# Turning four more pairs of attention heads by DMA, with another written order of steps, in a fused linear-attention and mixture-of-experts kernel

## Chip, cores and metric

The kernel runs on one core of a Trainium2 chip. The metric is the device time of one execution, in microseconds (us). A core has five engines that each run their own instruction list in order: TensorE (PE; its weight loads are PEld), VectorE (DVE), ScalarE (ACT), GpSimd (POOL) and SyncE (SP, which only issues DMAs here). They wait for each other through semaphores.

## The reference

Two stages are computed, one feeding the other.

```python
# attention: q, k, v are (8, 8, 576, 64), w_phi is (64, 128)
def phi(x):
    proj = einsum('bhsd,df->bhsf', x, w_phi)
    proj = proj - max(abs(proj), axis=-1)
    return concatenate([exp(proj), exp(-proj)], axis=-1)
kv  = einsum('bhsf,bhsd->bhfd', phi(k), v);  z = sum(phi(k), axis=2)
num = einsum('bhsf,bhfd->bhsd', phi(q), kv)
x   = num / (einsum('bhsf,bhf->bhs', phi(q), z) + 1e-6)      # -> (4608, 512)
# experts: w_gate (512, 8), w1 (8, 512, 1024), w2 (8, 1024, 512)
P = exp(x @ w_gate - max)
8 times:  P /= P.sum(1) + 1e-9;  P /= P.sum(0) + 1e-9;  P *= N / E
out = sum over e of  P[:, e:e+1] * (relu(x @ w1[e]) @ w2[e])
```

## The kernel before, in words

**Attention.** The 8 batches have 8 heads each, taken two at a time: a *pair*, numbered 0 to 31 (4 * batch + pair). 512 of the 576 positions of a head are worked off as four tiles of 128; the other 64 positions, the *rests*, go once per batch (`rest_a`, `rest_c`). For each pair `pair_a` projects the tokens of k (PE, `tokens`), takes the maxima of absolute values (DVE, L614), exponentials (ACT, L618) and scales v by them (POOL, L810); `maxima` and `queries`, which it returns, do the same for q. `pair_b` multiplies keys by values (PE, L622, copied by DVE in L892); its inner function `outs` forms numerator and denominator of one head (PE, L905) and divides on DVE (L913, L918, L919). The result lies in a buffer `xb`, tokens by features.

**Turning the output.** The experts need x with the features on the partitions, in the tile `xT`. `pair_c` does that for one pair. It has two ways: four PE transposes into a PSUM bank (L934) and a DVE copy to `xT` (L937); or one DMA transpose on SP's queue straight from `xb` to `xT` (L928). The kernel before uses the DMA for the pairs of batches 3 to 6.

**Experts.** xT is cut into nine groups of 512 tokens: group g below 8 is the main part of batch g, group 8 holds all rests. `gate` makes the logits of a group. Expert 0 is computed plainly (`up0`, `down0`) and needs no routing weight for most groups, so its matmuls can be put between attention steps: up0 of group g needs all four pairs of batch g in xT, and the weights that `load_w0` brings. They are the *fill* that keeps PE occupied while ACT and DVE work on attention. `routing` is a chain on DVE with one small matmul per round. Experts 1 to 7 follow with fast-multiplication schemes (`up7`, `up49`, `down7`), whose order of steps is written in `UNITS`.

**What sets the order.** Operations are recorded by `plan.op` with an engine, a cost and the keys that they read and write. `Plan.schedule` then places them: at each step it takes the operation that can start earliest by its costs, and of equals the one that was recorded first. So the recorded order matters, and for attention it is written by hand as a string of letters, `order`, one per step: l and e load, t turns q and k by DMA (L567), w loads expert 0's weights, r is `rest_a`, a, q and p the three parts of `pair_a`, b, n and m those of `pair_b`, c is `pair_c`, g is `rest_c` with `gate`, u and d are a quarter of `up0` or `down0` for a group. The n-th occurrence of a letter is its n-th piece of work. Loads (`stage_l`, `stage_e`, `load_w0`) also wait for the latest maxima that stand before them in the string (`gates`).

q and k of batches 0 and 1 come through SP and are turned on PE (L752); those of the others are cast by POOL's loads (L550) and turned by SP (L567). SP issues its DMAs in order, and so does POOL, between its computations: what waits holds up what stands behind it in the queue.

Of the kernel before, what the change touches and what calls it, by code (L numbers as in the profile page):

```python
# [349 lines left out]
def kernel(  # L350
# [18 lines left out]
    NP = H // 2  # L369
# [43 lines left out]
    def pe(cols, fn, r=(), w=(), takes=()):  # L413
        plan.op("PE", max(cols / 2400.0 + 0.0025, 0.031), 0.22, fn, r, w, takes)
# [4 lines left out]
    def dve(el, fn, r=(), w=(), shared=False):  # L419
        plan.op("DVE", el / 960.0 + 0.07, 0.15, fn, r, w, shared=shared)  # L420
# [7 lines left out]
    def dma(queue, nbytes, rate, fn, r=(), w=()):  # L428

        speed, unit = LINK.get(rate, (rate, 40))  # L430
        if nbytes == 2 << 20:
            speed, unit = 400, 150
        o = plan.op(queue, 0.8 if queue == "POOL" else 0.6, 0.0, fn, r, w, (), nbytes / speed)
        o.turn, o.unit = rate == 148, unit
# [71 lines left out]
    def new(tag):  # L506
        return R[tag].new()

    def bf(buf):

        return buf().bitcast(BF16)
# [412 lines left out]
        return xb, outs  # L924

    def pair_c(b, pr, xb):
        if b in (3, 4, 5, 6,):
            dma("SP", 1 << 17, 148, lambda: nc.sync.dma_start_transpose(  # L928
                out=xT[:, pr, b * SM:(b + 1) * SM].rearrange("p (a c) -> p a c", c=128),
                in_=xb()[:, 0:NJ].rearrange("p a b -> p (a b)")), [(xb, 0), (xb, 1)], [("xT", b, pr)])  # L930
            return
        pxt = new("PP")
        for j in range(NJ):
            pe(128, lambda j=j: nc.tensor.transpose(  # L934
                bf(pxt)[:, j * 128:j * 128 + 128], xb()[:, j, :], ident),
                [(xb, 0), (xb, 1), "ident"], [pxt])
        dve(270, lambda: nc.vector.tensor_copy(  # L937
            out=xT[:, pr, b * SM:(b + 1) * SM], in_=bf(pxt)[:, 0:512]),
            [pxt], [("xT", b, pr)])
# [150 lines left out]
    def stage_g(b):  # L1090
# [7 lines left out]
             "r": stage_r, "b": stage_b,  # L1098
             "n": lambda j: kvs[j](0), "m": lambda j: kvs[j](1),
             "c": lambda j: pair_c(j // 4, j % 4, xbs[j]), "g": stage_g,  # L1100
             "u": lambda i: up0(i // 4, i % 4), "d": lambda i: down0(i // 4, i % 4)}
    order = (
        "lraeaepqbwlqaqawwabwmqlltnrbppnwqbppmrmanbqaqmwwacmpnpbccpwbtcnmqnaqbclupunm"
        "taumquglcapalbcpnqqdcenmucugbblnapmrcqdutabnqpmunpbambccddnqplanmqmducpblttb"
        "augnaqlnrbdcampcadmqeutunqcppmdcaqtdqabpbbmlrqtdnpmuaqualbnagnacctbmqulupran"
        "tdpmtdqcmdnpdabdancpcabbqmpumqbcdgnappqunburqcbugmmnqdcdanumupqbnucmcpnmbddp"
        "bqmpncncubncmmgccg"
    )
    for i, n in enumerate(order):
        at[0] = i  # L1110
# [948 lines left out]
```

## Time and profile before

| what | value |
|---|---|
| runs, median of 3 | 1009.96 us (1009.75 to 1012.1) |
| profiled execution, first to last instruction | 1008.8 us |
| DMA moved | 128.86 MB, mean 128 GB/s |
| HBM read and written | 122.50 MB and 19.53 MB |
| granted TensorE clock | 1.000 over the whole span |

The span runs from the first to the last instruction of the profiled execution; the times of the runs are about 1.2 us longer, for what lies around the span. Busy time of an engine is the union of its instructions' records. PE records overlap, since matmuls are pipelined: a row such as "x8" merges eight neighbours, and its length less one record, divided by seven, is the step from one to the next. In rows of windows the columns are PE, PEld, DVE, ACT, POOL (busy us, and instructions in brackets), granted clock, mean share of DMA engines that are busy, and GB/s. In rows of the timeline they are the start, the length, engine, line, operation, output and inputs. Attention and the first fill take the first 204 us, routing and the rest of expert 0 last until about 259 us, and the other seven experts until the end.

### The profile page before, as it was taken

To read this page: it belongs to the slowest core of one execution; us is meant where nothing else is said; L and a number is where in the kernel's file an instruction comes from. 1 tells how busy PE (TensorE), PEld (TensorE's weight loads), DVE (VectorE), ACT (ScalarE), POOL (GpSimd) and SP (SyncE) were. 2 spreads that over 40 slices of the span, in tenths; PEclk is the share of its full clock that TensorE was granted. 3 is DMA by queue.
4 is the path that set the end of the run, shared out by engine and by line. 5 is a ranking of instruction groups with operands and counts; after the bars stand their busy time and mean duration, and the time that the engine had idled before them with its cause. 6 is when DMAs were issued, how large, how long until landed. Compare 5 with 4: busy or idle time off the path is not lost.

```text
span 1008.8 us, 23309 instructions
## 1 busy us (share of the span) xinstructions
PE 994.0 (99%) x8376; PEld 727.7 (72%) x8376; DVE 898.6 (89%) x1999; ACT 812.8 (81%) x1930; POOL 447.6 (44%) x514
## 2 busy tenths in 40 slices
PE   7899999999999999999999999999999999999998
PEld 5666666644566877777777877787778777787775
DVE  7999998987888998899989898989889988989886
ACT  7999999845979788878878788777887888778874
POOL 5778674400133344434444444444443444344443
PEclk9999999999999999999999999999999999999999
DMA  9999999181136423282327133632246222724653
GB/s 249 183 202 183 157 153 144 38 170 56 53 121 143 147 97 98 84 184 96 109 98 170 44 100 131 130 127 98 97 117 177 97 98 84 147 79 142 208 174 126
DMA packets 129748, 128.86 MB, mean 128 GB/s; under 512 B 55776, under 2 KB 98272, under 8 KB 129632
## 3 DMA queue, kind: packets, MB, share of 16 engines
q1 hardware_dynamic: 97680, 103.33, 36.3%
q0 software_dynamic: 31648, 23.86, 16.9%
q8 instruction: 65, 1.06, 0.5%
q14 instruction: 51, 0.42, 0.2%
q10 hardware_dynamic: 304, 0.20, 0.1%
HBM read 122.50 MB, written 19.53 MB: 141 GB/s over the span
## 4 chain that ended last, share of the span: by engine, by line
PE 92%; DVE 3%; ACT 2%; DMA 2%; issue 1%; POOL 0%; DVEq 0%
PE ps L1466 41%; PE ps L1475 20%; PE ps L622 17%; PE ps L1607 11%; PE ps L905 2%; DMA xi6t<-X 1%; DMA xi<-X 1%; PE ps L752 1%; ACT q L618 0%; DVE m L614 0%; ACT k L618 0%; DVE wx L614 0%; DVE X L1240 0%; DMA acc<-in_k_dram 0%; DVE hs L1676 0%
## 5 line engine op out<-in xcount | busy, mean ns | idle before, releaser
L1875 POOL TENSOR_TENSOR acc<-acc,hx 128x512 f32<-128x512 f32 x186 | 236.1, 1276 | 404.7 <-ACT hx L1872 135.0
L1466 PEld LDWEIGHTS <-hs 128*128 128x128 bf16 x1984 | 194.1, 98 | 46.4 <-issue 0.2
L1872 ACT ACTIVATE hx<-ps,P 128x256 f32<-128x256 f32 x372 | 158.9, 483 | 53.4 <-PE ps L1466 52.0
L1860 DVE SCALAR_TENSOR_TENSOR acc<-ps,P,acc 128x256 f32<-128x256 f32 x372 | 162.2, 478 | 30.2 <-PE ps L1466 28.2
L1475 PE MATMUL ps<-xT,T 128*128 128x512 bf16 x608 | 171.0, 379 | 0.0
L1466 PEld LDWEIGHTS <-hx 128*128 128x128 bf16 x1488 | 145.6, 98 | 24.9
L1466 PE MATMUL ps<-hx,hs 128*128 128x256 bf16 x992 | 144.3, 273 | 0.0
L1676 DVE CUSTOM_DVE_ANT_0 hs<-ps,U 128x512 bf16<-128x512 f32 x192 | 124.7, 684 | 11.3 <-PE ps L1475 6.6
L1607 PE MATMUL ps<-xT 128*128 128x256 bf16 x576 | 125.4, 272 | 0.0
L1475 PEld LDWEIGHTS <-T 128*128 128x128 bf16 x672 | 65.8, 98 | 40.6
L1682 ACT ACTIVATE hs<-ps 128x512 bf16<-128x512 f32 x96 | 55.9, 598 | 41.7 <-PE ps L1475 40.2
L1466 PE MATMUL ps<-wx,hs 128*128 128x256 bf16 x560 | 78.4, 273 | 0.0
L622 PE MATMUL ps<-w,hx 128*128 128x512 bf16 x288 | 73.0, 379 | 0.0
L622 PE MATMUL ps<-xT,w 128*128 128x512 bf16 x288 | 72.9, 379 | 0.0
L1466 PE MATMUL ps<-wx,hx 128*128 128x256 bf16 x496 | 72.3, 273 | 0.0
L1676 DVE CUSTOM_DVE_ANT_0 hs<-ps,X 128x512 bf16<-128x512 f32 x96 | 65.1, 684 | 7.8 <-PE ps L1607 6.9
L1466 PE MATMUL ps<-hx 128*128 128x256 bf16 x496 | 71.2, 273 | 0.0
L1607 PEld LDWEIGHTS <-xT 128*128 128x128 bf16 x576 | 56.3, 98 | 17.5
L1466 PE MATMUL ps<-w,hx 128*128 128x256 bf16 x432 | 62.2, 273 | 0.0
L614 DVE TENSOR_REDUCE m<-ps 128x4 f32<-128x512 f32 x88 | 58.8, 680 | 3.7 <-PE ps L622 1.9
L1672 ACT COPY X<-ps 128x512 f32<-128x512 f32 x96 | 58.6, 610 | 2.5 <-DVE ps L1650 2.5
L1466 PE MATMUL ps<-w,hs 128*128 128x256 bf16 x432 | 60.2, 273 | 0.0
(174 smaller groups left out, 2256.0 us busy)
## 6 DMA issues: line engine op xcount, KB each, us to landing
xT<-xi SPq DMA_DIRECT2D x48, 448.0 KB, 4.6
xT<-xd SPq DMA_DIRECT2D x72, 256.0 KB, 4.0
wx<-in_moe_w_dram POOLq DMA_DIRECT2D x8, 1024.0 KB, 11.2
v_m<-in_v_dram SPq DMA_DIRECT2D x15, 512.0 KB, 5.2
out_dram<-acc SPq DMA_DIRECT2D x14, 512.0 KB, 3.0
w<-in_moe_w_dram POOLq DMA_DIRECT2D x6, 1024.0 KB, 11.0
xT<-xp SPq DMA_DIRECT2D x24, 256.0 KB, 2.8
qk<-in_k_dram POOLq DMA_DIRECT2D x12, 256.0 KB, 5.4
```

The costliest lines, as they stand in the source:

```text
L614: dve(el, lambda: nc.vector.tensor_reduce(out=dst(), in_=src(), axis=AX.X, op=ALU.max, apply_absolute_value=True), r, w)
L622: nc.tensor.matmul(out_, lhsT=lhsT, rhs=rhs, start=start, stop=stop)
L905: pe(65, lambda j=j: nc.tensor.matmul(pn()[:, j * D1:j * D1 + D1], lhsT=s["T"][x]()[:, j % 2, 2 * h + j // 2, :] if j < 4 else r["T"][x]() ...
L1466: pe(256, lambda i=i, k=k, z=z: nc.tensor.matmul(bank()[:, 256 * i:256 * i + 256], lhsT=lhs(k, i), rhs=rhs(k), start=first and z, stop=k = ...
L1475: pe(512, lambda k=k: nc.tensor.matmul(bank().rearrange("p (a b) -> p a b", a=2), lhsT=lhs(k), rhs=rhs(k), start=first and k == 0, stop=k ...
L1607: pe(256, lambda: nc.tensor.matmul(halves_of(bank[q], n)(), lhsT=lhs(), rhs=t()[:, rhs, :], start=start, stop=True, skip_group_check=True) ...
L1672: act(512, lambda: nc.scalar.copy(out=flat(to[q])(), in_=bank[q]()), [bank[q]], [(to[q], 0), (to[q], 1)])
L1676: dve(515, lambda: nc.vector._custom_dve(ADD_SAT, out=out_(q, i, j), in0=bank[q]().rearrange("p (a b) -> p a b", a=2), in1=to[q](), s0=3.0 ...
L1682: act(512, lambda: nc.scalar.activation(out=out_(q, i, j), in_=bank[q]().rearrange("p (a b) -> p a b", a=2), func=ACT.Relu, bias=0.0, scal ...
L1860: dve(320, lambda n=n, ts=ts: nc.vector.scalar_tensor_tensor(out=acc[g][:, ts, 256 * j:256 * j + 256], in0=bank()[:, 256 * n:256 * n + 256 ...
L1872: act(370, lambda n=n: nc.scalar.activation(out=u()[:, n, :], in_=bank()[:, 256 * n:256 * n + 256], func=ACT.Copy, bias=0.0, scale=P[:, 4 ...
L1875: pool(695, lambda: nc.gpsimd.tensor_tensor(out=acc[g][:, 2 * i:2 * i + 2, 256 * j:256 * j + 256], in0=acc[g][:, 2 * i:2 * i + 2, 256 * j: ...
```

## The change

It does two things. `pair_c` takes the DMA way for pairs 10 to 29 instead of 12 to 27: two pairs of batch 2 and two of batch 7 more, 20 of 32 in all. And the string of steps is another one, with the same 322 letters, each as often as before.

```diff
     def pair_c(b, pr, xb):
-        if b in (3, 4, 5, 6,):
+        if 2 * NP + 2 <= NP * b + pr < 7 * NP + 2:
             dma("SP", 1 << 17, 148, lambda: nc.sync.dma_start_transpose(
...
     order = (
-        "lraeaepqbwlqaqawwabwmqlltnrbppnwqbppmrmanbqaqmwwacmpnpbccpwbtcnmqnaqbclupunm"
-        "taumquglcapalbcpnqqdcenmucugbblnapmrcqdutabnqpmunpbambccddnqplanmqmducpblttb"
-        "augnaqlnrbdcampcadmqeutunqcppmdcaqtdqabpbbmlrqtdnpmuaqualbnagnacctbmqulupran"
-        "tdpmtdqcmdnpdabdancpcabbqmpumqbcdgnappqunburqcbugmmnqdcdanumupqbnucmcpnmbddp"
-        "bqmpncncubncmmgccg"
+        "llreaqbaappwqnqlbaqmwnwbrcapnwbmmccwpeqbwaqwamtppapnwlbcqlqbgunmnpamlncaueqr"
+        "ubtuqtntacpmbmccnamlqupabnatmabuacpunqupddcgprlqtdbmpmanleqbdllmdpqaqbcacunr"
+        "nduappqcbbmndtbculqanqutmrqcgbbpmmqdndpbdcprmmutantcgnplbnduqapcbalumcqdnuqc"
+        "bantmpupqcnbbntmaddaqpmqugampuqdcapaaqdmcubcrbmndqpdmnbnudapmbqdpnmncqucbgnb"
+        "pcbmmcucnupnmcgccg"
     )
```

Both of batch 1's loads now stand at the front of the string, ahead of the first `rest_a` and of the rests' loads; the loads of the rests of batches 2 and 3 (`stage_e(1)`) have moved from the sixth place to the thirty-eighth; the first gate and the first fill step come at places 61 and 62 instead of 83 and 72.

## The prediction, made before the changed kernel had run

> **What bounds the kernel now.** I read the page first: the busy table, the chain that ended last, then the windows of the span, then single rows of the timeline.
>
> ```profile
> span 1008.8 us, 23309 instructions
> PE 994.0 (99%) x8376; PEld 727.7 (72%) x8376; DVE 898.6 (89%) x1999; ACT 812.8 (81%) x1930; POOL 447.6 (44%) x514
> PE 92%; DVE 3%; ACT 2%; DMA 2%; issue 1%; POOL 0%; DVEq 0%
> ```
>
> TensorE (PE) is busy 99% of the span and holds 92% of the chain. A busy PE can still hide gaps, because a matmul's record is longer than the step to the next one, so I take steps from merged rows. One step is (row length minus one record) over (count minus one).
>
> ```profile
> 207.40 1.89 PE L622 MATMUL ps<-xT,w 128*128 128x512 bf16 x8
> 44.06 0.60 PE L622 MATMUL ps<-wphi,qkT 128*128 128x256 bf16 x4
> 43.54 0.68 PE L622 MATMUL ps<-v,k 128*128 128x65 bf16 x16
> 202.27 0.39 PE L934 MATMUL ps<-ident,wx 128*128 128x128 bf16 x4
> 202.49 0.22 PE L944 MATMUL ps<-ident,xb 128*128 128x128 bf16 x1
> 3.99 1.99 PE L752 MATMUL ps<-identf,acc 128*128 128x128 f32 x8 [3.99 <-DMA acc<-in_k_dram]
> 7.91 2.11 PE L752 MATMUL ps<-identf,acc 128*128 128x128 f32 x8
> 871.36 25.22 PE ps L1466 x231
> ```
>
> A 512-column matmul steps by (1.89-0.38)/7 = 0.216 us, a 256-column one by 0.110, a 65-column one by 0.033. Four bf16 transposes take 202.49-202.27 = 0.22 us, so one takes 0.055 us. The last row is a piece of the chain far behind the change: 231 matmuls of 256 columns in 25.22 us, 0.109 each, which is the bare step. There PE never waits. Where it does wait is shown by the windows (PE, PEld, DVE, ACT, POOL, clock, DMA share, GB/s):
>
> ```profile
> 0.00:3.90 3.90, 0.00 (x0) 0.00 (x0) 2.16 (x4) 1.58 (x2) 0.68 (x6) 1.00 0.55 141
> ...
> 0.00:25.00 25.00, 18.52 (x157) 12.62 (x157) 19.63 (x38) 19.42 (x47) 13.42 (x27) 1.00 1.08 248
> 25.00:45.40 20.40, 17.52 (x193) 12.32 (x193) 19.91 (x44) 20.29 (x54) 14.90 (x27) 1.00 1.30 195
> 45.40:60.00 14.60, 14.23 (x183) 9.71 (x181) 14.56 (x37) 14.60 (x38) 13.55 (x20) 1.00 1.20 212
> 60.00:100.00 40.00, 40.00 (x486) 26.90 (x485) 37.88 (x92) 37.90 (x94) 30.39 (x49) 1.00 1.21 177
> 150.00:204.00 54.00, 54.00 (x692) 35.95 (x690) 48.10 (x118) 49.27 (x116) 25.06 (x42) 1.00 0.53 86
> 258.80:1008.80 750.00, 745.27 (x5863) 573.33 (x5861) 670.57 (x1465) 593.36 (x1414) 313.60 (x294) 1.00 0.42 120
> 45.42 0.43 DVE L937 COPY xT<-ps 128x512 bf16<-128x512 bf16 x1
> 45.48 0.38 PE L622 MATMUL ps<-xT,w 128*128 128x512 bf16 x1
> PE ps L752 <- DMA acc<-in_k_dram: 4.0, 1, 4.0
> ```
>
> Until 45.5 us VectorE (DVE) and ScalarE (ACT) set the pace: from 25 to 45.4 us they are busy 98% and 99%. At 45.42 DVE starts the fourth copy that completes batch 0 of xT, and at 45.48 PE starts its first expert-0 matmul, the fill that keeps it occupied between attention steps. The 349 matmuls ahead of that one are 80 + 80 of 65 columns, 72 of 256, 72 fp32 transposes at 0.110, 19 of 512, 16 bf16 transposes and 10 of 130 columns (0.057): 2.6 + 2.6 + 7.9 + 7.9 + 4.1 + 0.9 + 0.6 = 26.6 us. So PE has stood still for 45.5 - 26.6 = 18.9 us by then, 4.0 of them for the first load (the last row, from the view of waits, where it is the only wait of PE for a DMA). From 60 us on it is packed. Hence the time is PE's work plus what it stands still early, and anything that costs PE nothing and delays nothing it needs is free.
>
> **The change part by part.** The profiled execution lasts 1008.8 us by its span; the median of the runs is 1009.96, so about 1.2 us lie around the span, and I keep that difference. In the program as built, the changed kernel has the same instructions but for these: 16 transposes (L934) and four copies (L937) fewer, four DMA transposes (L928) more. From about 258 us on, all 5,864 matmuls stand in the same order. So everything happens in the first quarter.
>
> *Transposes off PE.* 16 x 0.055 = 0.88 us. Batch 2's two pairs stood in 80 to 90 us, batch 7's from 194 us on (rows below); PE is packed in both stretches, so I count them in full: **-0.9 us**. The Trainium skill, page "VectorE: DVE Perf Modes", section "The three transpose paths", prices a 128x128 bf16 transpose at 390 ns on TensorE; 16 of them would be an estimated 6.2 us. The trace disagrees: four share 0.22 us.
>
> ```profile
> 88.83 0.39 PE L934 MATMUL ps<-ident,xb 128*128 128x128 bf16 x4
> L934 PE MATMUL ps<-ident,xb x40: 216/218/222, 37.9 to 194.2; 128*128 128x128 bf16 x40
> L937 DVE COPY xT<-ps x16: 384/415/426, 41.2 to 202.7; 128x512 bf16<-128x512 bf16 x16
> L928 SPq DMA_TRANSPOSE xT<-xb x10: 1189/1195/1723, 94.5 to 188.4; - x10
> DMA to landing us min/median/max: 2.3/4.6/7.2
> 39.53 0.68 DVE L614 TENSOR_REDUCE m<-ps 128x4 f32<-128x512 f32 x1
> 40.12 0.19 DVE L918 RECIPROCAL rec<-ps 128x5 f32<-128x5 f32 x1
> ```
>
> *Copies off DVE.* 4 x 0.415 = 1.7 us of DVE, worth nothing on the path while PE covers it: in 60 to 100 us DVE has 2.1 of 40 us idle and PE none. If that cover were gone they would be worth at most that 1.7 us.
>
> *The written order before the first fill.* The built order has the first fill matmul behind 346 matmuls instead of 349: four 256-column and three 512-column ones fewer, four transposes of the rests more, 0.44 + 0.65 - 0.22 = 0.87 us less. On DVE the fourth xT copy stands behind 79 instructions instead of 81; the two that left are maxima (L614) with a step of 40.12-39.53 = 0.59 us, so it comes 1.2 us earlier. The first fill moves to about 44.3 us, with 25.7 us of work ahead: PE stands still 18.6 instead of 18.9. **-0.3 us.** Bounds: the batch-1 rests are now loaded behind 1.05 MB of q and k (4.2 us at 248 GB/s) and may arrive late for rest_a(1), at most +1; on the other side DVE idles 5.4 us of the first 25, 1.7 of them before the first load has come, and a denser start could win up to the other 3.6.
>
> *Loads moved.* On POOL, the loads of the second half of batch 2 now stand behind the seventh scaling of v (L810), the last of them behind the eighth. These rows price it:
>
> ```profile
> 51.46 1.93 POOL L810 TENSOR_TENSOR v<-v_m,em 128x1024 bf16<-128x1024 f32 x1
> 54.47 1.92 POOL L810 TENSOR_TENSOR v<-v_m,em 128x1024 bf16<-128x1024 f32 x1
> DMA to landing us min/median/max: 4.2/5.8/8.0
> DMA to landing us min/median/max: 4.3/5.8/10.3
> ```
>
> The last two are the loads of q and k (L550) and their turn by DMA (L567). The eighth scaling ends between 53.5 (its input, em from ACT, stands 2.9 us of ACT work further forward in the built order) and 56.4 (as in the trace); plus 5.8 and 5.8, the turned half is there at 65 to 68 us. Its first use, pair 10's tokens, has 46.3 us of PE work ahead in the built order, by the steps above; with 18.6 us of standing still and 1 to 2 more in the thin stretch from 45 to 60, it comes near 66.5. So 0 to +1.5 us, and nothing to win, since PE waits for none of these loads now; I take **+0.3**, near the lower end, as half of the interval lies before the use.
>
> *Four DMA transposes added.* Pairs 10 and 11 feed the first fill of group 2. Before, that was this:
>
> ```profile
> 87.63 0.48 DVE L919 TENSOR_TENSOR xb<-ps,wx 128x320 bf16<-128x320 f32 x1
> 89.56 0.41 DVE L937 COPY xT<-ps 128x512 bf16<-128x512 bf16 x1
> 94.87 1.89 PE L622 MATMUL ps<-xT,w 128*128 128x512 bf16 x8
> 85.00 5.99 SPq L686 DMA_TRANSPOSE rT<-qk_r  x2
> 203.36 0.94 PE L622 MATMUL ps<-wgate,xT 128*128 128x8 bf16 x32
> ```
>
> Pair 11's last scaling ends at 88.1, the copy starts at 89.56, the fill reads it from 94.87. In the built order the scaling has 0.3 us less DVE work ahead (87.8), the fill 1.8 us less PE work; its matmuls on pairs 10 and 11 come near 93.5. That leaves 5.7 us for the transfer: the median landing of 4.6 fits, the longest of 7.2 would be 1.5 late. 0 to +1.5; I take **+0.2**. The transfer also holds the SP queue: v loads and qk turns stand behind it, and who needs those is POOL's scaling and PE's tokens several pairs on. At 177 GB/s two pieces of 131 KB delay the other loads by 1.5 us, hidden while these have that much spare. Pairs 28 and 29 are needed by the last gates, now near 202.3 us; by the same count pair 29 is scaled near 195.8 and lands near 200.4, with the DMA engines half idle there: no cost, at most 0.7.
>
> **The sum.** -0.9 - 0.3 + 0.3 + 0.2 = -0.7: span 1008.1, time **1009.3 us**.
>
> **The rivals.**
>
> *A turned piece comes late (slower).* The place is group 2's first fill near 93.5 us. If SP is held by two turns when pair 11 is ready, as in the row at 85.00 (5.99 us), and the landing takes 7.2, the piece is there at 87.8 + 6.0 + 7.2 = 101.0, and PE, in order, stands 7.5 us: 1009.1 + 7.5 = **1016.6**. PE waits from 5.7 us between scaling and landing on; the kernel is 3 us slower than before from about 9.6 us on. For it: DMA share over 1 from 60 to 100 us. Against it: the 16 transfers of before landed in 7.2 at most, and PE waits for none of them. The same page of the Trainium skill, section "Rules for kernel authors", says to transpose 128x128 on TensorE where PSUM can take it, and gives the DMA path 1309 ns against 390; this rival is what that rule would do here. That the DMA way takes longer agrees with the trace (4.6 us to landing against 0.22 us and one copy); whether anyone waits, the page cannot say.
>
> *The start gets denser (faster).* If the new order closes the 3.6 us that DVE idles after the first load, the first fill comes at 40.7 and the time is 1009.3 - 3.6 = **1005.7**. For it: steps changed places from the second letter on. Against it: the same DVE and ACT work, already 98% busy from 25 us, leads to the fill.
>
> *Nothing reaches the end.* The 0.9 us turns into new short stops, as a share of the 0.4 us that PE lacks in 45 to 60 us already: **1010.0**.
>
> **How the numbers follow.** A measurement of this kernel can tell about 0.3%, 3 us, from no change. The forecast gets 0.51, nothing at the end 0.25 (both within 0.3%: 0.76), the late piece 0.14, the denser start 0.10. The likely cases' terms together span -0.9 - 0.3 = -1.2 to -0.9 + 1.0 + 1.5 + 1.5 = +3.1, that is 1008.8 to 1013.1, of which all three delays at once is improbable. Reaching into both rivals until no more than 2 in 10 is left out, the range is 1006.5 to 1012.8.
>
> **What would show it.** PE rows: 48 transposes at L934, none between 80 and 190 us; first fill at 44.3 us, first tokens of pair 10 near 66 and group 2 near 92.5 without an idle time put down to DMA; the stretch after 258 us shifted and otherwise the same. A PE wait on a DMA at 66, 93 or 202 us, or a first fill after 45.5, makes the prediction wrong.

## The result, and the profile after

| kernel | median us | lowest to highest | runs |
|---|---|---|---|
| before | 1009.86 | 1009.52 to 1012.1 | 6 |
| changed | 1017.73 | 1015.38 to 1020.51 | 6 |

The ratio is 1.0076, 95% interval 1.0061 to 1.0090: the changed kernel is 7.9 us slower. Its profiled run is the fastest of its six: 1015.38 us, span 1013.6.

The view of waits of PE in the changed kernel (us in total, times, longest):

```profile
PE ps L622 <- DMA qkT<-qk: 5.3, 2, 3.5
PE ps L752 <- DMA acc<-in_k_dram: 3.8, 1, 3.8
...
PE ps L622 <- DMA xT<-wx: 0.2, 1, 0.2
```

Before, PE waited for one DMA only, the first load. Now it also waits twice for turned q and k, 5.3 us. The timeline of PE says where:

```profile
43.00 0.59 PE L622 MATMUL ps<-xT,w 128*128 128x512 bf16 x2 [0.21 <-DVE m L614]
...
90.80 0.59 PE L622 MATMUL ps<-xT,w 128*128 128x512 bf16 x2
...
117.35 1.70 PE L622 MATMUL ps<-wphi,qkT 128*128 128x256 bf16 x14 [1.82 <-DMA qkT<-qk]
...
131.21 1.89 PE L622 MATMUL ps<-wphi,qkT 128*128 128x256 bf16 x8 [3.48 <-DMA qkT<-qk]
```

The first fill starts at 43.0 instead of 45.5 us, and group 2's fill, the place that the rival named, starts at 90.8 with no wait for the added transposes. The two waits are at the first tokens of pair 18 (half (4,1) of q and k) and of pair 20 (half (5,0)). The eight matmuls of the last row take 1.89 us; at their bare step of 0.11 they would take about 1.0. The windows show why (PE, PEld, DVE, ACT, POOL, clock, DMA share, GB/s):

```profile
60.00:100.00 40.00, 39.83 (x457) 26.29 (x454) 37.03 (x85) 39.62 (x99) 27.64 (x47) 1.00 0.97 153
...
115.20:117.30 2.10, 0.33 (x5) 0.02 (x1) 1.07 (x3) 0.71 (x3) 0.41 (x3) 1.00 3.08 158
...
127.50:131.30 3.80, 0.32 (x5) 0.16 (x4) 0.61 (x2) 0.71 (x3) 0.17 (x2) 0.91 1.28 181
131.30:135.00 3.70, 3.70 (x37) 2.74 (x38) 2.36 (x5) 2.28 (x5) 1.57 (x2) 0.64 1.27 282
...
258.80:1008.80 750.00, 749.08 (x5879) 574.90 (x5878) 671.33 (x1466) 599.12 (x1424) 313.97 (x294) 1.00 0.41 120
```

After the second wait the granted clock is 0.64 in the window from 131.3 to 135 us. From 258.8 us on PE is packed, so what was lost by then stays lost: counted from the end, matmul 5,864 starts 5.2 us later than in the kernel before, and the last ones 5.0 us.

What PE waited for, from the chain of waits between 95 and 140 us (start and length of each link, here from a turn's issue to its landing):

```profile
105.26 12.04 DMA qkT<-qk
...
118.72 12.44 DMA qkT<-qk
```

The same two turns in the kernel before, on SP's timeline:

```profile
91.16 1.78 SPq L567 DMA_TRANSPOSE qkT<-qk  x1
...
103.04 2.96 SPq L567 DMA_TRANSPOSE qkT<-qk  x1
```

They were issued 14 and 16 us earlier and landed at 95.4 and 107.8 us, 14.4 and 11.4 us ahead of their first use. In the changed kernel they land at 117.3 and 131.2, when PE has been waiting for them. Landing times here and below are read from the trace's DMA records. The delay starts with POOL: the loads of these two halves were issued from 81.0 and 94.0 us on before, and from 99.1 and 106.1 us on in the changed kernel. And there is company in flight; POOL's timeline of the changed kernel:

```profile
106.11 0.81 POOL L550 DMA_DIRECT2D qk<-in_k_dram  x1 [0.26 <-issue]
108.94 0.81 POOL L550 DMA_DIRECT2D qk<-in_q_dram  x1
109.75 0.70 POOL L605 DMA_DIRECT2D qk_r<-in_k_dram  x1
```

The new string places the q and k loads of (5,0) and all loads of the last rests (`stage_e(3)`) between the load of (4,1) and its use.

### The profile page after: what moved, and what is told of

It is laid out like the page before. It is cut to its first block, busy times and chain, and to the rows that moved or that the text cites. A ratio compares the mean times of both kernels' runs of the same rounds, so it can differ in the third digit from the quotient of the medians.

```text
span 1013.6 us, 23270 instructions
## 1 busy us (share of the span) xinstructions
PE 992.4 (98%) x8360; PEld 727.5 (72%) x8360; DVE 897.0 (88%) x1995; ACT 812.6 (80%) x1930; POOL 447.7 (44%) x514
## 4 chain that ended last, share of the span: by engine, by line
PE 89%; DMA 4%; DVE 3%; ACT 2%; issue 1%; POOL 1%; SPq 0%; DVEq 0%
PE ps L1466 41%; PE ps L1475 20%; PE ps L622 16%; PE ps L1607 11%; DMA qkT<-qk 2%; PE ps L905 2%; DMA xi6t<-X 1%; DMA xi<-X 1%; DMA acc<-in_q_dram 1%; ACT q L618 0%; ACT k L618 0%; ACT wx L618 0%; DVE m L614 0%; DVE X L1240 0%; DVE ps L913 0%
## 5 line engine op out<-in xcount | busy, mean ns | idle before, releaser
L622 PE MATMUL ps<-xT,w 128*128 128x512 bf16 x288 | 74.0, 379 | 0.4 <-DMA xT<-wx 0.2
L622 PE MATMUL ps<-w,hx 128*128 128x512 bf16 x288 | 73.6, 379 | 0.0
```

What stands on the lines that cost most here:

```text
L622: nc.tensor.matmul(out_, lhsT=lhsT, rhs=rhs, start=start, stop=stop)
```

## Experiments

Theory A: the new order issues turns of q and k so late that any slow landing stops PE. Theory B: the four added DMA transposes slow what shares SP's queue or the DMA engines. The first two kernels change one line or one string and are planned anew. In all others the plan is kept, and single operations are exchanged or moved, so that one thing changes at a time.

### Each part alone, planned anew

```diff
 e1_new_string (the changed kernel)
-        if 2 * NP + 2 <= NP * b + pr < 7 * NP + 2:
+        if b in (3, 4, 5, 6,):
 e2_old_string (the kernel before)
-        if b in (3, 4, 5, 6,):
+        if 2 * NP + 2 <= NP * b + pr < 7 * NP + 2:
```

> The new string of steps with the old condition in pair_c (16 pairs turned by DMA, as before). Theory A (the new string issues the loads and turns of q and k late and in a bunch): the slow-down stays, 1014 to 1020 us, PE waits for qkT for 3 us or more between 100 and 140 us. Theory B (the four added DMA transposes do it): about 1009 to 1011 us, and no wait of PE for qkT over 1 us.

> The old string with the new condition (20 pairs turned by DMA). Theory A: as fast as the kernel before or up to 0.9 us faster, 1008.8 to 1010 us, no wait of PE for qkT. Theory B: 1014 to 1018 us, with PE waiting for turned q and k behind the added transposes.

Measured: the new string alone 1033.67 us, ratio 1.0228 (1.0205 to 1.0251); the new condition alone 1014.88, ratio 1.0052 (1.0035 to 1.0069). One PE row of each:

```profile
127.82 1.04 PE L622 MATMUL ps<-wphi,qkT 128*128 128x256 bf16 x4 [4.82 <-DMA qkT<-qk]
```

```profile
97.38 1.91 PE L622 MATMUL ps<-xT,w 128*128 128x512 bf16 x5 [2.75 <-DMA xT<-xb]
```

The first has the wait that A expects, but its time lies far above A's range, and this wait does not account for it: PE waits 9.2 us for DMAs after the first load, and the run is 16.5 us behind the kernel before at 230 us and 22.4 us at 377 us, behind attention, where the new plan has another order too. The second has the time that B expects, with PE waiting for pair 11's piece at group 2's fill and not for q and k. Either part alone loses, each at its own place, and neither theory explains both. Since each plan is a new one, the parts had to be separated with the plan kept.

### The four transposes in the old order

In `pair_c` of the kernel before, pairs 10, 11, 28 and 29 keep their place in the plan, but the copy becomes the DMA transpose and the PE transposes go; then only 28 and 29; then all but 11.

```diff
+        turned = NP * b + pr in (10, 11, 28, 29)      # e9: (28, 29); e15: (10, 28, 29)
...
-            pe(128, lambda j=j: nc.tensor.transpose(
+            pe(128, lambda j=j: None if turned else nc.tensor.transpose(
...
-        dve(270, lambda: nc.vector.tensor_copy(
+        dve(270, lambda: nc.sync.dma_start_transpose(
+            out=xT[:, pr, b * SM:(b + 1) * SM].rearrange("p (a c) -> p a c", c=128),
+            in_=xb()[:, 0:NJ].rearrange("p a b -> p (a b)")) if turned else nc.vector.tensor_copy(
...
```

> The kernel before with nothing changed but pairs 10, 11, 28 and 29: in the place of each xT copy stands a DMA transpose on SP, the four PE transposes are gone, and all other instructions keep their order. Theory A2: 0.9 us less PE work and at most a short wait at group 2's first fill near 94 us: 1009 to 1010.5 us. Theory B: the transposes delay the turns behind them on SP, or group 2's fill waits 3 us or more: 1012 to 1016 us.

> The kernel before with only pairs 28 and 29 turned by DMA, in the place of their copies. If all of the 7.4 us that the four cost in place comes from group 2's first fill (pairs 10 and 11): no wait of PE for a DMA after 5 us, 1009.3 to 1010.3 us, within 0.1% of the kernel before. If transposes cost wherever they stand: 1012 us or more.

> As the run with the four in place, but pair 11 stays with PE and DVE: pairs 10, 28 and 29 by DMA. If only the piece that is scaled last before group 2's fill has too little time: no wait of PE for a DMA after 5 us, 1009 to 1010.5 us. If pair 10's transpose delays the turn of half (4,1) and with it POOL's loads: PE waits for v near 100 us, 1011 us or more.

Measured: four in place 1017.61 us, ratio 1.0073 (1.0058 to 1.0088); two late ones 1010.57, ratio 1.0002 (0.9993 to 1.0011); without pair 11 1010.31, ratio 1.0008 (0.9993 to 1.0024), seven of its ten runs at 1009.3 to 1010.7 and three at 1015.1 to 1016.2. SP's queue with the four in place, and PE:

```profile
85.48 5.37 SPq L686 DMA_TRANSPOSE rT<-qk_r  x2
90.94 1.22 SPq L938 DMA_TRANSPOSE xT<-xb  x1
92.32 1.32 SPq L567 DMA_TRANSPOSE qkT<-qk  x1
93.77 1.92 SPq L938 DMA_TRANSPOSE xT<-xb  x1
```

```profile
101.45 2.29 PE L622 MATMUL ps<-xT,w 128*128 128x512 bf16 x5 [6.66 <-DMA xT<-xb]
```

Two turns of rests hold SP for 5.37 us, pair 11's transpose is issued at 93.77, lands at 101.4, and PE stands still for 6.66 us at group 2's fill. That is the rival's mechanism within a microsecond (piece at 101.0, 7.5 us of standing still) in the old order. The three longer runs without pair 11 show another wait, as far as the one that was profiled tells; POOL's timeline of it:

```profile
100.44 0.81 POOL L550 DMA_DIRECT2D qk<-in_k_dram  x1 [3.95 <-DMA qkT<-qk]
...
102.00 1.94 POOL L810 TENSOR_TENSOR v<-v_m,em 128x1024 bf16<-128x1024 f32 x1
```

POOL's load needs the buffer that the turn of (4,1) frees; it waits 3.95 us, and the scaling of v, for which PE waits 3.5 us, stands behind it in POOL's list.

### SP's queue reordered

Still the four in place; in `Plan.run` operations are moved in the finished plan. The numbers name operations in the order of their recording: 1435 and 1440 are pairs 10 and 11, 2061 and 1716 the turns of rests, 1598 the turn of (4,1), 967 the load of v.

```diff
+        for n, after in MOVES:
+            done.remove(self.ops[n])
+            done.insert(done.index(self.ops[after]) + 1, self.ops[n])
# e10  MOVES = ((1435, 1334), (1440, 1410), (1598, 1440), (2061, 1440), (1716, 1440))
# e13  MOVES = ((1435, 1334), (1440, 1410), (967, 1274), (1598, 967), (2061, 967), (1716, 967))
# e14  MOVES = ((1435, 1334), (1440, 1410), (2061, 1598), (1716, 1598))
```

> As the run with the four in place, but on SP the transposes of pairs 10 and 11 stand ahead of both turns of rests (L686) and of the turn of half (4,1), which are first needed 14 us and more later. If the order of SP's queue made pair 11 late: it is issued near 88 to 89 us and lands by 94, PE waits under 1 us at group 2's fill, no half clock, 1009 to 1010.5 us. If the load on the DMA engines made it late: it lands after 96 and PE still waits 2 us or more, 1012 to 1016 us.

> As the run with the reordered SP queue, and the load of v that stood behind the turn of half (4,1) (L558) goes ahead of it and of both turns of rests too. If each wait came from what stands ahead on SP: pair 11 lands by 94 us, v by 99 us, PE waits under 1 us in all between 90 and 105 us, and what is left is 0.9 us less PE work: 1008.8 to 1010.3 us, the four DMA transposes then cost nothing in the old order. If the DMA engines cannot carry the two pieces there in any order: another transfer is late, PE waits 3 us or more, 1012 us or more.

> As the run with the reordered SP queue, but the turn of half (4,1) keeps its place and only the two turns of rests (L686) go behind it: SP issues pair 10, pair 11, the turn, the two turns of rests, the load of v. In the two reordered runs POOL stood 7.4 and 9.5 us behind its own load of q and k (L550), which needs the buffer that this turn frees, and the scaling of v (L810) stood behind that load. If that is what cost 7 us and more there: the turn is issued near 92 us and lands near 97, POOL waits under 2 us, pair 11 lands by 94.5, PE waits under 1 us: 1008.8 to 1010.5 us. If the DMA engines cannot carry the pieces in any order: 1012 us or more.

Measured: 1016.96 us, ratio 1.0072 (1.0058 to 1.0085); 1021.35, ratio 1.0102 (1.0085 to 1.0119); 1012.18, ratio 1.0022 (1.0011 to 1.0033). In the first, pair 11 lands at 94.0 and group 2's fill does not wait, but POOL does; in the second I had taken the load of v for the cause, and that was wrong: v lands at 98.1 in time, and POOL waits longer. POOL of the first, the second and the third:

```profile
104.55 0.81 POOL L556 DMA_DIRECT2D qk<-in_k_dram  x1 [7.35 <-DMA qkT<-qk]
105.36 0.76 POOL L556 DMA_DIRECT2D qk<-in_q_dram  x1
106.11 1.93 POOL L816 TENSOR_TENSOR v<-v_m,em 128x1024 bf16<-128x1024 f32 x1
```

```profile
109.04 0.81 POOL L556 DMA_DIRECT2D qk<-in_k_dram  x1 [9.54 <-DMA qkT<-qk]
```

```profile
96.92 0.81 POOL L556 DMA_DIRECT2D qk<-in_k_dram  x1 [0.32 <-issue]
```

(In these three kernels the added code shifts L550 to L556, L622 to L628 and L810 to L816.) The turn of (4,1) itself may not go back: its first use is 14.7 us off, but its landing frees the buffer for a POOL load with a v scaling behind it, for which PE waited 6.8 and 9.0 us. With the turn kept in its place and only the two turns of rests behind, all four pieces come in time, and 5.4 of the 7.4 us are won back. What is left is 2.0 us of the median. The profiled run (1011.45 us) lies 0.4 us ahead of the kernel before until 106 us and 1.4 us behind it at 111 us. PE waits in between for no DMA, but for ACT; its waits, and two links of the chain that leads to them:

```profile
PE ps L628 <- ACT q L624: 1.9, 3, 1.2
...
97.11 8.04 DMA v_m<-in_v_dram
...
107.68 1.56 ACT q L624 x3
```

Between these two links stands POOL's scaling of v. The load of v now stands behind the two turns of rests; it lands at 105.1 us, in the kernel before at 98.1. So the order that brings pair 11 in time makes this load late.

### The clock

```diff
 e12_in_place_filled: ahead of the first matmul of up0(2, 0), on its bank
 e8_pe_filled: ahead of the first tokens of pair 20, 28 instead of 56
...
+                for _ in range(56):
+                    mm(ph()[:, 0:256], wphi2f[:, 0:128], wphi2f, True, True)
```

> As the run with the four in place, with 56 extra matmuls of 256 columns (6.1 us by 0.109 each) ahead of group 2's first fill matmul; they write a bank that this matmul then starts anew. If a standstill of some us brings half clock and this costs of its own: the wait of PE shrinks to about 0.6 us, granted clock stays 1.00 from 97 to 105 us, and the time falls by 1 to 2 us, to 1015.5 to 1016.7 us. If the clock costs nothing: 1017.3 to 1018 us.

> The changed kernel with 28 extra matmuls of 256 columns (3.05 us by 0.109 each) ahead of the first tokens of pair 20, where PE stands still 3.6 us near 127.5 us; their result is written over. If the stretch at half clock follows from the standstill and costs about 1.7 us of its own: granted clock 1.00 near 131 us, and the profiled execution ends about 1.7 us earlier than the changed kernel's at an equal landing of the turn, 1014 to 1018 us as median. If the half clock has another cause: it stays, and the time is the changed kernel's or up to 3 us more where a run has no such wait.

Measured: 1017.84 us (1017.13 to 1018.39), ratio 1.0077 (1.0064 to 1.0090), against 1017.61 (1017.02 to 1018.12) unfilled; and 1016.28 (1012.91 to 1019.17), ratio 1.0058 (1.0036 to 1.0080), against the changed kernel's 1017.73. Windows of the four in place, unfilled and filled:

```profile
97.00:101.00 4.00, 0.00 (x0) 0.00 (x0) 0.00 (x0) 0.00 (x0) 1.56 (x2) 0.54 1.25 166
...
101.30:104.50 3.20, 3.05 (x13) 1.25 (x13) 0.00 (x0) 1.32 (x3) 0.00 (x0) 0.56 1.32 230
```

```profile
97.00:101.00 4.00, 4.00 (x39) 3.48 (x37) 0.48 (x1) 0.00 (x0) 1.56 (x2) 1.00 1.44 87
101.00:104.50 3.50, 2.56 (x23) 1.33 (x22) 0.00 (x0) 1.30 (x3) 0.00 (x0) 1.00 1.30 263
```

And the second wait of the changed kernel, filled:

```profile
127.53 3.22 PE L622 MATMUL ps<-wphi 128*128 128x256 bf16 x28
...
131.79 1.05 PE L622 MATMUL ps<-wphi,qkT 128*128 128x256 bf16 x8 [1.03 <-DMA qkT<-qk]
```

The half clock does follow from the standstill: filled, the clock stays at 1.00. What it costs shows when the runs are laid on the kernel before, matmul by matmul. Unfilled, the first matmul after the wait starts 5.93 us later than there, and the distance has grown to 7.24 us when the clock is full again: 1.3 us. Filled, it is 7.01 us at both places. The changed kernel loses 1.3 us in the same way between 131.2 and 134 us (row e8 of the table of starts below: 0.58 to -0.69). So the clock costs 1.3 us at each such place, somewhat less than my price of 1.7, and the wait itself is the larger loss. The medians do not show the gain: in the profiled filled kernel pair 11 landed at 102.5 instead of 101.4 us, and the interval of e8 overlaps the changed kernel's. The Trainium skill, page "TensorE: Matmul & The Clock Gate", part 1, says that the clock is halved after at least one idle window of about 3.4 us; the record of the granted clock shows halves of 3.4 us, which agrees, but here shorter standstills were enough (below).

### The new order, with the plan kept

`hoist` in `Plan.run` takes an operation of the changed kernel forward in the finished plan to a given place, though never ahead of what it reads or of the last use of its buffer. e3 moves the six loads of the last rests, e4 four loads and two turns of q and k, e5 twelve loads (of six halves) and five turns, e6 those of e5 and the rests' loads. e11 keeps every place and puts a copy by POOL, which does not turn the piece, where each of the four added transposes was; four pieces of x are then not transposed.

```diff
+    def hoist(self, done, o, mark):
+
+        at = done.index(o)
+        held = {(id(b.ring), b.slot) for b in o.bufs if not b.ring.psum}
+        to = max([mark] + [i + 1 for i, x in enumerate(done[:at]) if (
+            x in o.deps and (o.turn or x.eng != "DVE")) or any(
+            (id(b.ring), b.slot) in held and b not in o.bufs for b in x.bufs)])
...
+        done.insert(to, done.pop(at))
# e3  MOVES = ((1426, 1453), (1428, 1460), (1427, 1480), (1431, 1490), (1429, 1500), (1430, 1510))
# e4  MOVES = ((1324, 1325), (1325, 1335), (1334, 1455), (1423, 1460), (1424, 1480), (1751, 1590))
 e11_new_no_dma, in pair_c behind the recorded transpose
+            if b in (2, 7):
+                plan.ops[-1].fn = lambda: nc.gpsimd.tensor_copy(
+                    out=xT[:, pr, b * SM:(b + 1) * SM],
+                    in_=xb()[:, 0:NJ].rearrange("p a b -> p (a b)"))
```

> The changed kernel in its own order, but the four added pieces are copied by POOL without being turned (0.9 us each), so the four added DMA transposes are gone from SP's queue and from the DMA engines; x has four pieces that are not transposed. Theory A (the new order makes the turns of q and k late): PE still waits for the turns of (4,1) and (5,0) near 115 and 127 us, 1014 to 1020 us. Theory B (the added transposes load the engines in the new order too): these waits go, 1009 to 1011 us.

> The changed kernel with the six loads of the last rests (L605 four times, L607 twice) issued some 15 to 20 us earlier, near 88 to 92 us instead of 104 to 112; all else in the same order on each engine. Theory A in its narrow form (these six loads are what makes the bunch): the turns of the halves (4,1) and (5,0) land in 5 to 8 us instead of 12, PE waits for qkT less than 1 us in all, no stretch at half clock near 131 us, 1008 to 1011 us. If the q and k loads and turns are late by themselves: the two turns still land after 113 and 126 us, and the time stays within 2 us of the changed kernel's. Theory B: no change.

> The changed kernel with the loads of q and k of halves (4,1) and (5,0) (L550, four of them) and their two turns (L567) moved forward in the lists of POOL and SP: loads near 81 and 89 us instead of 99 and 106, turns near 89 and 98 us instead of 105 and 119. The rests' loads and the added transposes stay where they are. Theory A: PE no longer waits for qkT, no stretch at half clock, 1007 to 1010 us. Theory B: the added transposes still hold the queue, and the waits move to another turn, 1014 us or more.

> The changed kernel with the loads of q and k of six halves, (2,1) and (4,1) to (6,1), and the turns of (2,1) and (4,1) to (6,0) moved forward in the lists of POOL and SP by 6 to 20 us, as far as their buffers are free; everything else in the same order. Theory A2 (what the new string lost is the time between the landing of a turn and its first use; any slow landing then stops PE): every turn has at least 4 us to its first use, PE waits for qkT under 0.5 us, no half clock, 1007 to 1010 us, with runs closer together than the changed kernel's 1015.4 to 1020.5. Theory B (the added transposes): no gain, 1015 us or more.

> As the run with all q and k early, and the last rests' loads near 94 to 96 us as well. Theory A2: the rests' turn (rT) has more time too; 1006.5 to 1009 us, below the kernel before. If the loads only compete with each other wherever they stand: no better than the run with q and k early alone, or worse.

| kernel | median us | lowest to highest | ratio to before, 95% |
|---|---|---|---|
| changed | 1017.73 | 1015.38 to 1020.51 | 1.0061 to 1.0090 |
| e11, without the four DMA transposes | 1015.61 | 1014.35 to 1016.14 | 1.0040 to 1.0066 |
| e3, rests' loads earlier | 1011.94 | 1008.86 to 1016.76 | 0.9999 to 1.0029 |
| e4, two halves earlier | 1015.60 | 1013.31 to 1018.17 | 1.0035 to 1.0072 |
| e5, all q and k earlier | 1014.67 | 1012.43 to 1015.29 | 1.0026 to 1.0055 |
| e6, both | 1016.02 | 1012.34 to 1018.23 | 1.0026 to 1.0070 |

e3 wins back 5.8 us of the changed kernel's median, more than any other of these. PE's waits in e11: without the added transposes the waits for qkT remain, in sum and rows:

```profile
PE ps L622 <- DMA qkT<-qk: 4.6, 3, 2.0
...
66.65 0.61 PE L622 MATMUL ps<-wphi,qkT 128*128 128x256 bf16 x4 [1.19 <-DMA qkT<-qk]
...
130.30 1.05 PE L622 MATMUL ps<-wphi,qkT 128*128 128x256 bf16 x8 [1.96 <-DMA qkT<-qk]
...
150.47 0.61 PE L622 MATMUL ps<-wphi,qkT 128*128 128x256 bf16 x4 [1.50 <-DMA qkT<-qk]
```

They are not all at the old places: the rows are the first tokens of the halves (2,1), (5,0) and (6,0). But the turns of (4,1) and (5,0) land at 117.3 and 130.3 us, as late as in the changed kernel (117.3 and 131.2); PE does not wait for (4,1) here because it comes 0.9 us later itself. So the added transposes do not make these turns late, and the new order alone, without one more DMA transpose, is 5.5 us slower than before: A. In e3, whose added code shifts L622 to L637, the tokens of pair 18 no longer wait, though its profiled run, the slowest of ten, waited elsewhere:

```profile
57.82 1.04 PE L637 MATMUL ps<-wphi,rT 128*128 128x256 bf16 x4 [3.51 <-DMA rT<-qk_r]
...
122.27 1.69 PE L637 MATMUL ps<-wphi,qkT 128*128 128x256 bf16 x14
```

In e4 neither pair 18 nor pair 20 waits (no bracket in their rows of PE's timeline), but the halves (2,1), which lies ahead of all that e4 moves, and (6,0) do (PE's waits):

```profile
118.55 1.69 PE L637 MATMUL ps<-wphi,qkT 128*128 128x256 bf16 x14
...
128.66 1.03 PE L637 MATMUL ps<-wphi,qkT 128*128 128x256 bf16 x8
```

```profile
PE ps L637 <- DMA qkT<-qk: 2.4, 2, 1.6
```

In e5 the wait has gone to group 3's fill, to a piece of x of batch 3 that both kernels turn by DMA; in e6 to the weights and to POOL's scaling:

```profile
126.42 0.97 PE L637 MATMUL ps<-xT,w 128*128 128x512 bf16 x3 [1.94 <-DMA xT<-wx]
```

```profile
PE ps L637 <- POOL wx L831: 1.9, 1, 1.9
PE ps L637 <- DMA w<-in_moe_w_dram: 1.4, 1, 1.4
```

Because these kernels run the same matmuls in the same order, each can be laid on the changed kernel: the start of the same matmul, less its start there, in us (from the PE rows of both traces).

```
at (changed kernel)    70     111     117     131     134     143     200     864
e3                    6.90    6.90    4.92    1.24   -0.04    0.46    2.24    1.40
e4                    2.51    3.18    1.20   -2.54   -3.83   -3.81   -1.77   -2.09
e5                    1.73    3.11    1.13    0.45   -0.83   -0.82   -0.82   -0.80
e8                    1.08    1.06   -0.01    0.58   -0.69   -0.68   -0.68   -1.49
e11                   2.49    2.87    0.89   -0.91   -2.18   -1.58    1.32    0.24
```

Read a row from left to right; 117 and 131 are the first matmuls behind the two waits, and at 134 the clock is full again. From 111 to 134 us, e3 falls by 6.9 and e4 by 7.0 us: that is what the two late turns cost in the changed kernel, 2.0 at the first, 3.6 at the second and 1.3 by the clock behind it. From 134 to 200, e3, e4 and e11 give 2.1 to 3.5 us back, at turns that come later, at a piece of x and behind POOL. And the first column: up to 80 us e3, e4, e8 and e11 have the changed kernel's instructions in its order, and yet are 1.1 to 6.9 us later at 70 us than its profiled run. In the old order the kernels with the instructions of before up to about 84 us lay -0.8 to +0.3 us from its profiled run at 76 us, one of them (e13) +2.6.

Two sources of this scatter can be read. e3 waited for the turn of the rests (the row at 57.82), e4 and e11 for the turn of half (2,1). And the start itself varies with the clock. The same eight fp32 transposes, in the changed kernel and in e8, which has the same instructions there:

```profile
7.56 1.39 PE L752 MATMUL ps<-identf,acc 128*128 128x128 f32 x8
```

```profile
7.78 2.25 PE L752 MATMUL ps<-identf,acc 128*128 128x128 f32 x8
```

The trace's record of the clock begins at 7.7 us in the first and at 10.4 us in the second, at full clock. Ahead of it the views give 1.00, but the steps are double: about 0.25 us a transpose in the second row, against 0.110 later on.

## Why the prediction was wrong

*What failed.* The step "Loads moved", +0.3; in its place the runs show 6.9 to 7.0 us at two late turns. The step looked at one half, (2,1), because there the new order issues loads later than the old, and found it just in time; in the profiled run that was right (its turn landed at 63.6, its first tokens started at 64.2), and in e4 and e11, with the same instructions up to there, PE waited 1.6 and 1.2 us for it, inside the 0 to 1.5 of the step but for 0.1. It did not count the same distance, from landing to first use, for the other turns of q and k. In the kernel before it is 2.5 us and more for each turn after 60 us, 14.4 and 11.4 for (4,1) and (5,0); in the changed kernel it is below zero for these two. What these turns stand behind in the built order of SP and POOL could be read there; I did not read it. The sentence that what stands behind the added transposes is "hidden while these have that much spare" named the condition and did not check it; in the new order it was the order itself that took the spare time (e11).

*Transposes off PE*, -0.9: the count was right, the gain too high where it can be seen. In the old order the kernel with the four in place is 0.84 us ahead of before at 84 us, which belongs to its start, and 0.89 at 91 us: the eight transposes of pairs 10 and 11 gave 0.05 us, for 0.44 forecast. PE reached the next steps sooner and then stood there, 0.19 us of it for DVE at 85 us. The two late pairs gave 0.2 to 0.3 us by 203 us, for 0.44. PE was not packed in the sense that the step took; part of the gain turned into new short stops, as the prediction's own "Nothing reaches the end" has it. In the new order no run separates this term.

*The order before the first fill*, -0.3: not refuted. The fill came at 43.0, not 44.3, with 1.6 us less standing still. But in e3, e4, e8 and e11, which have the same instructions up to there, it came at 43.3, 43.8, 44.1 and 44.1, so the early fill of the profiled run is in part luck; e8's clock was full 2.7 us later. By 70 us these four are up to 7 us later. The rows of the first ten us also show a misreading of mine: the 72 fp32 transposes were taken at 0.110 us each, while those at 3.99 and 7.91 take about 0.25, so the 26.6 us of work are some 2 us too few and the 18.9 us of standing still as much too many.

*Four DMA transposes added*, +0.2: right for the place that I worked out (group 2's fill at 90.8, no wait). For all four it is not settled: e11 puts them at about 2 us of the median (1017.73 against 1015.61), but the intervals touch and e11 has four POOL copies in their place.

*The late piece* (1016.6, chance 0.14): the mechanism and price were right for the old order (6.66 us of waiting, 1017.61), where I had read its rows. In the new order, group 2's fill did not wait, and PE stood 25 us later for other pieces that came late. That the time came out near the rival's 1016.6 is luck.

*The sum.* In the two profiled runs: -1.6 before the first fill (25.7 us of work in 43.0, against 26.6 in 45.5), -0.3 to -0.9 by the transposes, +6.9 to +7.0 by the two turns: +4.4 to +5.1, and the spans differ by 4.8 us. The median of the changed kernel lies 2.4 us above its profiled run; that this is the scatter of the first 70 us is argued from the four kernels above, since no second run of it was profiled.

*Theories.* A is shown for the new order (e11, e3), B for the old one (e7). They look like one case: in the windows above between 60 and 135 us the share of busy DMA engines is 0.97 to 3.08, most often above 1, and in every order that was tried another transfer came late. That the order alone decides which one is argued, not shown. Neither A's hope that early turns cure it (e4, e5, e6) nor an order of SP that makes the four free (e10, e13, e14) held: a moved transfer made another one late. No version's median beat the kernel before.

## What to carry to other kernels

Where PE is packed and DMA is busy, list for each transfer the time between its landing and its first use, in the new order too, and count its landing at the longest, not at the median; the shortest distance is the bound. Ask also who waits for the buffer that a transfer frees, and what stands behind that waiter on its engine. Taking 0.9 us off a busy engine is worth nothing if it puts a transfer where the distance is 5 us; and a busy engine can give the time back at its next short stop, so the gain itself is to be measured.

## What the runs showed of the hardware

The landing of one 512 KB turn by DMA (L567) varied from 4.2 to 15.6 us over these kernels; the changed kernel's own row (least, median, most):

```profile
DMA to landing us min/median/max: 4.6/7.3/12.4
```

With the rests' loads out of the way (e3) the two turns landed in 8.5 and 7.4 us instead of 12.0 and 12.4. The Trainium skill, page "DMA: Bandwidth & Descriptors", section "Issuing engines are not separate DMA queues", says that DMAs of all issuers share 16 engines and interleave; the turns on SP slowed by POOL's loads agree with it.

A standstill of PE much shorter than 3.4 us can bring half clock, but it depends on where it falls. The 1.94 us in e5 were followed by this window, while the 1.96 us in e11 (the row at 130.30) and the 1.82 us of the changed kernel's first wait were not followed by any half clock.

```profile
126.50:130.00 3.50, 3.50 (x35) 2.48 (x35) 1.37 (x4) 2.33 (x5) 3.06 (x6) 0.56 1.47 183
```

In the clock records of the 17 traces the stretches inside the span last 3.41 us or a multiple of it, so the clock changes on a grid of 3.41 us. With the grid laid back from each record, e5's standstill lies in one window of it, and e11's is cut by a boundary into 1.38 and 0.58 us. Over all these traces, PE's idle time was summed in each window at full clock, from the record's first entry to the end of the span less 2 us: the 12 windows with 1.89 us or more were each followed by half clock, and none with 1.55 us or less was.
